# A dense feed-forward layer that takes 512 tokens at a time instead of 256

## The chip, the cores and the metric

The kernel runs on one core of a Trainium2 chip. The metric is the device time of one execution in microseconds (us); the kernel before has a median of 1231.29 us over three runs (1230.88 to 1233.56). Engines are named as in the profile: PE is TensorE (matmuls), PEld its weight loads, DVE is VectorE, ACT is ScalarE, POOL is GpSimd and SP is SyncE, whose queue issues most DMAs.

## What is computed

Attention over 4 x 8 heads (queries are first averaged in pairs) gives `x` with 2304 tokens of 512 numbers. A dense feed-forward layer follows, with w_in of 512 x 2048 and w_out of 2048 x 512, and then a layer of 8 experts in which each token goes to one:

```
h = x @ w_in
x = (h * cos(h)) @ w_out                      # dense feed-forward

expert = argmax(x @ w_gate);  p = softmax(x @ w_gate)[expert]
out = p * (relu(x @ w1[expert]) @ w2[expert])
```

## The kernel before, in words

Numbers are kept in float32 precision by splitting an operand into a high part (`xh`, rounded by a copy to the matmul's type) and a low part (`xl`, the rest). Each product is three matmuls: high by high, high by low, low by high. The splitting copy is done by ACT, the subtraction by DVE.

Three stages follow each other on PE: attention (to 480.83 us of the profile), the dense layer (to about 914), the experts (to about 1220). The attention leaves x transposed in SBUF (`xT`), as 9 chunks of 256 tokens, and converts w_in and w_out into their two parts, through memory (`ws`).

The dense layer is in `moe`. The outer loop takes a chunk `c` of 256 tokens, the inner loop `f` 16 slices of 128 of the 2048 hidden numbers. A step (c, f) is one `layer1`, and one `layer2` that lies four steps behind (LAG):

- `layer1` (L859): 12 matmuls of 256 moving columns into a PSUM bank `h` (four banks), the weights stationary, L870. Then a chain on ACT and DVE forms h cos(h): L875 scales and rounds on ACT, L876 to L878 reduce the argument on DVE, L879 takes a sine and L880 squares it on ACT, L881 multiplies by h on DVE, L882 (ACT) and L883 (DVE) split the result into `g`. `h` is read last by L881 and `g` is one of eight buffers. `a` and `r`, the values in between, share a 256 + 256 tile in SBUF.
- `layer2` (L886): 6 matmuls of 512 columns, L891, `g` stationary, into two PSUM banks `po` that collect the sum over the 16 steps.

Behind the last step of a chunk the `epilogue` runs in pieces, one piece a step: it copies `po` out (L804), transposes it on PE (L812), forms the expert scores (L820, L825) and lets the `Router` rank the tokens. In the last chunk the first expert's weights are converted as well (`conv`, L715 on ACT, L716 on DVE, 1024 columns each).

The text of the program is not the order of the instructions: the framework's scheduler moves them past each other on each engine within what data, buffers and its own estimates allow. Every engine then runs its own instructions strictly in the order so fixed, and waits where a semaphore tells it to.

The experts load raw weights through 9 buffers `raw` (L693, L706, L708), which in the earlier stages hold `xT`, convert them and multiply in `compute`.

Of the kernel before, what the change touches and what calls it, by code (L numbers as in the profile page):

```python
# [8 lines left out]
F32 = mybir.dt.float32  # L9
F32R = mybir.dt.float32r  # L10
# [3 lines left out]
AF = mybir.ActivationFunctionType  # L14
# [7 lines left out]
CH = 256  # L22
ROW = 512 + 8


# [151 lines left out]
def attention(nc, tc, q, k, v, xT, ident, w_in, w_out, ws, x2d, W1):  # L177
# [11 lines left out]
    with ExitStack() as ctx:  # L189
# [177 lines left out]
        def norm(i, hq):  # L367
            b, c = divmod(i, HP)
            t = t0 = b*SQ + hq*NQ
            o = T.pop(("ob", i, hq))  # L370
            while t < t0 + NQ:
                n = min(CH - t % CH, t0 + NQ - t)
                nc.gpsimd.tensor_mul(xT[t//CH][:, c, t % CH:t % CH+n], o[:, t-t0:t-t0+n], T["nr", i, hq][:, t-t0:t-t0+n])
                t += n
# [57 lines left out]
class Router:  # L432
# [51 lines left out]
    def bank(self, name):  # L484
        return self.ps.tile([128, 512], F32, tag="h", name=name)
# [163 lines left out]
def moe(nc, tc, magic, rp, xT, ws, w_gate, x2d, w1, w2, out, ident, W1, wp):  # L649
# [5 lines left out]
    NCH = NT // CH  # L655
    LAG = 4
    C1 = 6.28125
    C2 = 2 * math.pi - C1
    with ExitStack() as ctx:
        pool = lambda name, bufs, **k: ctx.enter_context(tc.tile_pool(name=name, bufs=bufs, **k))  # L660
        xhp = pool("xh", 3)
        xlp = pool("xl", 2)
        hp = pool("g", 8)
        op = pool("o", 4)
        wp = wp + [pool(f"w{j}", 1) for j in range(len(wp), FT)]
        cq = pool("cm", 1)
        gp = pool("gate", 3)
        x2p = pool("x2", 3)
# [3 lines left out]
        half = lambda name: ps_h.tile([128, 512], F32, tag="h", name=name)[:, :CH]  # L672
        bank = lambda name: ps_m.tile([128, 512], F32, tag="h", name=name)
# [9 lines left out]
        def xtiles():  # L683
            return [(xhp.tile([128, 2, CH], F32R, tag="xh", name="xh"), xlp.tile([128, 2, CH], F32R, tag="xl", name="xl")) for _ in range(KC // 2)]

# [7 lines left out]
        def load(i, part=range(8)):  # L693
            s = slots[i][1]
            src = router.e0 if i == 0 else router.eid[0:1, s:s+1]
            if part[0]:

                src = router.e1
                tc.keep_in_program_order(nc.gpsimd.tensor_copy(src, router.eid[0:1, s:s+1]))
            e = nc.sync.value_load(src, min_val=0, max_val=NE-1)  # L700
            RAW.setdefault(i, [])
            for j in part:
                t = rp.tile([128, 1024], F32, tag="raw", name="raw")
# [47 lines left out]
        def compute(i, between=()):  # L751
# [3 lines left out]
            if n == 2:  # L755
                for m in range(F2):
                    ph = half("ph")
# [5 lines left out]
                    h = hp.tile([128, 2, CH], F32R, tag="g", name="hh")  # L763
                    nc.scalar.activation(h[:, 0], ph, AF.Relu)
                    nc.vector.scalar_tensor_tensor(h[:, 1], ph, 0.0, h[:, 0], op0=ALU.max, op1=ALU.subtract)
                    hs.append(h)
            else:
                for u in range(2):
                    hr = otile("hr")
                    ph = ps_h.tile([128, 512], F32, tag="h", name="ph")  # L770
                    c = 0
                    for k in range(KC):
                        for a, y in ((0, 0), (0, 1), (1, 0)):
                            nc.tensor.matmul(ph, lhsT=x[k//2][y][:, k % 2, :128], rhs=wt[k][:, a, u*512:(u+1)*512], start=(c == 0), stop=(c == 3*KC-1))
                            c += 1
                    nc.scalar.activation(hr, ph, AF.Relu)
                    p = bank("ht")
                    for k in range(4):
                        nc.tensor.transpose(p[:, k*128:(k+1)*128], hr[:, k*128:(k+1)*128], ident)
                    for k2 in range(2):  # L780
                        h = hp.tile([128, 2, CH], F32R, tag="g", name="hh")
                        pv = p[:, k2*256:(k2+1)*256]
                        nc.scalar.copy(h[:, 0], pv)  # L783
                        nc.vector.tensor_sub(h[:, 1], pv, h[:, 0])
                        hs += [h[:, :, :128], h[:, :, 128:]]
            for q in range(n):
                po = ps_o.tile([128, D], F32, tag="po", name="po")
                c = 0
# [10 lines left out]

        def epilogue(c, po):  # L800
# [4 lines left out]
            yield  # L805
            if c < NCH-1:
                yield
            x2t = []
# [47 lines left out]

        tail, todo, xs, pos = [iter(())], [], {}, {}

        def layer1(c, f):  # L859
            if c == 0 and f >= EARLY:  # L860
# [4 lines left out]
            w, x = W1[f], xs[c]  # L865
            h = half("h")
            n = 0
            for k in range(KC):
                for a, y in ((0, 0), (0, 1), (1, 0)):
                    nc.tensor.matmul(h, lhsT=w[:, a, k*128:(k+1)*128], rhs=x[k//2][y][:, k % 2], start=(n == 0), stop=(n == 3*KC-1))  # L870
                    n += 1
            ar = op.tile([128, 2, CH], F32, tag="o", name="ar")
            a, r = ar[:, 0], ar[:, 1]
            g = hp.tile([128, 2, CH], F32R, tag="g", name="g")
            nc.scalar.activation(a, h, AF.Identity, bias=magic, scale=1.0/(2*math.pi))  # L875
# [8 lines left out]
            todo.append((c, f, g))  # L884

        def layer2(c, f, g):  # L886
            if f == 0:
                pos[c] = [ps_o.tile([128, D], F32, tag="po", name="po") for t in range(2)]
            for t in range(2):
                for i, (y, b) in enumerate(((0, 0), (0, 1), (1, 0))):  # L890
                    nc.tensor.matmul(pos[c][t], lhsT=g[:, y, t*128:(t+1)*128], rhs=W1[f][:, b, 512:], start=(f == 0 and i == 0), stop=(f == FT-1 and i == 2))  # L891
            if f == FT-1 and c < NCH-1:
                tail[0] = epilogue(c, pos.pop(c))

        xs[0] = xtiles()
        split_x(xs[0], xT[0])
        for c in range(NCH):
            for f in range(FT):
                layer1(c, f)
                while len(todo) > (LAG + 1 if f == LAG and c else LAG):  # L900
                    layer2(*todo.pop(0))
                next(tail[0], None)
                if c == 0 and f == 8:
                    router = Router(nc, cq, op, ps_m, NT // 128, NE)
                if c < NCH-1 and f == FT-2:
                    xs[c+1] = xtiles()
                    split_x(xs[c+1], xT[c+1])
                if c == NCH-1 and f >= 9:
                    conv(0, f - 9)
# [3 lines left out]
        split(0)  # L913
        for _ in epilogue(c, pos.pop(c)):
            pass
# [24 lines left out]
def body(nc, tc, q, k, v, w_in, w_out, w_gate, w1, w2, out):  # L940
    with ExitStack() as ctx:
# [9 lines left out]
        x2d = dp.tile([NT + 128, ROW], F32, name="x2d")  # L951
        rp = ctx.enter_context(tc.tile_pool(name="raw", bufs=NT // CH))
        xT = [rp.tile([128, 1024], F32, tag="raw", name="xT").rearrange("p (k n) -> p k n", n=CH) for c in range(NT // CH)]

# [43 lines left out]
```

## Time and profile before

| | us |
|---|---|
| median of 3 runs | 1231.29 |
| profiled execution | 1229.78 |
| its span, first to last instruction | 1228.1 |
| PE busy in the span | 1199.8 |
| DVE busy | 873.6 |
| ACT busy | 760.5 |
| POOL busy | 432.1 |

The difference between the profiled execution and its span, 1.7 us, lies around the first and last instruction. Busy time is counted per engine and engines overlap, so the shares do not add up to the span. The granted clock is 0.998 of full speed over the whole span. Within a stage, what matters is which engine has no idle time: a window of the trace tells that, and a timeline tells how far apart the instructions of a chain start. The chain that ended last goes back only to the last store and its issue (3 pieces), so it says nothing about the dense layer.

### The profile page before, as it was taken

What the parts mean: (1) busy time and instruction counts of PE and PEld (TensorE: products, weight loads), DVE (VectorE), ACT (ScalarE), POOL (GpSimd) and SP (SyncE); (2) the same over time, 40 slices, a digit from 0 to 9 for tenths busy, and PEclk for the clock granted to TensorE, in tenths of its full rate; (3) what the DMA queues carried; (4) which work ended last, traced back from release to release, by engine and by line L of the source; (5) the groups of instructions that cost most, each with busy time, mean ns of one, the idle gap of its engine ahead of it and who ended that gap; (6) DMA issues with size and microseconds to landing.
All of it is one profiled execution on the core that took longest, in us unless ns stands there. A gap on an engine that the chain in (4) does not pass through costs nothing. (4 is left out here: it accounts for less than half of the span.)

```text
span 1228.1 us, 22479 instructions
## 1 busy us (share of the span) xinstructions
PE 1199.8 (98%) x8286; PEld 937.3 (76%) x8286; DVE 873.6 (71%) x1895; ACT 760.5 (62%) x1528; POOL 432.1 (35%) x386
## 2 busy tenths in 40 slices
PE   5999999999999999999999999999998999999997
PEld 3566666666665556989889889889987888888886
DVE  4677777767777766767767767767777977777761
ACT  3566666666666666666566565565574877677751
POOL 4687888888888776000000000000003121112100
PEclk9999999999999999999999999999999999999999
DMA  6234464433433335600000000000047997779710
GB/s 257 74 95 147 176 221 147 151 128 127 127 132 108 118 105 223 258 19 1 18 19 1 19 1 18 19 1 19 21 153 256 399 328 267 271 274 313 259 58 7
DMA packets 70943, 163.74 MB, mean 133 GB/s; under 512 B 7669, under 2 KB 24813, under 8 KB 68784
## 3 DMA queue, kind: packets, MB, share of 16 engines
q1 hardware_dynamic: 66832, 150.92, 35.1%
q0 software_dynamic: 4000, 11.38, 2.5%
q8 instruction: 65, 1.06, 0.4%
q14 instruction: 46, 0.38, 0.1%
HBM read 135.65 MB, written 28.39 MB: 134 GB/s over the span
## 5 line engine op out<-in xcount | busy, mean ns | idle before, releaser
L334 POOL TENSOR_TENSOR es<-es,E 128x576 f32<-128x576 f32 x192 | 274.6, 1430 | 34.6 <-ACT E L327 24.6
L327 ACT ACTIVATE E<-s 128x576 f32<-128x576 f32 x288 | 183.4, 653 | 122.9 <-PE s L323 111.9
L870 PE MATMUL h<-xh,wf 128*128 128x256 f32 x1152 | 231.6, 285 | 0.5 <-DVE ar L881 0.5
L274 DVE TENSOR_REDUCE MX<-pmx 128x2 f32<-128x768 f32 x192 | 183.2, 957 | 68.4 <-PE pmx L263 68.4
L891 PE MATMUL po<-wf,g 128*128 128x512 f32 x864 | 222.3, 394 | 1.5 <-ACT g L882 0.9
L321 PE MATMUL s<-Q,K 64*128 64x288 f32 x1152 | 191.9, 417 | 1.5 <-ACT E L327 1.5
L870 PEld LDWEIGHTS h<-xh,wf 128*128 128x128 f32 x1152 | 188.1, 191 | 6.5 <-issue 1.8
L727 POOL DMA_INDIRECT xg<-x2d,idx x25 | 27.7, 1106 | 465.5 <-ACT ar L875 388.7
L891 PEld LDWEIGHTS po<-wf,g 128*128 128x128 f32 x864 | 153.4, 189 | 28.4 <-ACT g L882 1.6
L716 DVE TENSOR_TENSOR w<-raw,w 128x1024 fp32r<-128x1024 f32 x128 | 154.6, 1221 | 21.2 <-ACT w L715 15.5
L340 PE MATMUL o<-E,vt 128*64 128x288 f32 x1152 | 169.1, 417 | 0.2 <-ACT E L327 0.2
L870 PE MATMUL h<-xl,wf 128*128 128x256 f32 x576 | 163.0, 283 | 0.0
L323 PE MATMUL s<-MR,ON 64*128 64x288 f32 x576 | 148.4, 511 | 0.0
L715 ACT CAST w<-raw 128x1024 fp32r<-128x1024 f32 x128 | 132.9, 1053 | 20.1 <-DMA raw<-in_moe_w_dram 11.8
L794 PE MATMUL po<-w,hh 128*128 128x512 f32 x600 | 143.6, 392 | 0.4 <-ACT hh L783 0.3
L794 PEld LDWEIGHTS po<-w,hh 128*128 128x128 f32 x600 | 110.7, 188 | 22.6 <-ACT hh L783 0.8
L879 ACT ACTIVATE ar<-ar 128x256 f32<-128x256 f32 x144 | 59.9, 417 | 94.5 <-DVE ar L878 94.1
L340 PEld LDWEIGHTS o<-E,vt 128*64 128x64 f32 x1152 | 72.0, 136 | 59.9 <-issue 24.8
L321 PEld LDWEIGHTS s<-Q,K 64*128 64x128 f32 x1152 | 97.7, 188 | 25.2 <-issue 13.4
L870 PEld LDWEIGHTS h<-xl,wf 128*128 128x128 f32 x576 | 110.0, 191 | 3.7
L761 PE MATMUL ph<-xh,w 128*128 128x256 f32 x576 | 109.2, 286 | 1.2 <-ACT xh L688 1.2
L881 DVE SCALAR_TENSOR_TENSOR ar<-ar,h 128x256 f32<-128x256 f32 x144 | 60.2, 419 | 61.0 <-ACT ar L880 60.5
(200 smaller groups left out, 1808.0 us busy)
## 6 DMA issues: line engine op xcount, KB each, us to landing
raw<-in_moe_w_dram SPq DMA_DIRECT2D x128, 512.0 KB
wf<-ws SPq DMA_DIRECT2D x16, 1024.0 KB
vt<-in_v_dram SPq DMA_DIRECT2D x16, 576.0 KB
qr<-in_q_dram SPq DMA_DIRECT2D x15, 576.0 KB
K<-in_k_dram SPq DMA_DIRECT2D x15, 576.0 KB
cv_t<-in_moe_w_in_dram SPq DMA_DIRECT2D x16, 512.0 KB
ws<-cv_o SPq DMA_DIRECT2D x32, 256.0 KB
cv_t<-in_moe_w_out_dram SPq DMA_DIRECT2D x16, 512.0 KB
```

The source lines that it names most:

```text
L274: nc.vector.reduce_max(out.rearrange("p (w g) -> p w g", g=3)[:, 2*t:2*t+2, g], p[:, :, :KG], axis=AX.X)
L321: nc.tensor.matmul(p[:, h, :NQ], lhsT=T["k", i][R[h], j*128:(j+1)*128], rhs=T["q", i][R[h], qs], start=True, stop=False)
L323: nc.tensor.matmul(p[:, h, :NQ], lhsT=ON[R[h]], rhs=MR[i % 3][R[h], qs], start=False, stop=True)
L327: nc.scalar.activation(e, T.pop(("s", i, hq, j))[:, :, :NQ], AF.Exp, scale=1.0/16)
L334: nc.gpsimd.tensor_add(T["es", i, hq], T["e", i, hq, 0] if j == 1 else T["es", i, hq], T["e", i, hq, j])
L340: nc.tensor.matmul(T["o", i, hq][64*h:64*h+64], lhsT=T["v", i][:, h, j], rhs=T["e", i, hq, j][:, h], start=(j == 0), stop=(j == J-1))
L715: nc.scalar.copy(w[:, 0], t)
L716: nc.vector.tensor_sub(w[:, 1], t, w[:, 0])
L761: nc.tensor.matmul(ph, lhsT=wt[k][:, a, m*128:(m+1)*128], rhs=x[k//2][y][:, k % 2], start=(c == 0), stop=(c == 3*KC-1))
L794: nc.tensor.matmul(po, lhsT=hs[m][:, y, q*128:(q+1)*128], rhs=wt[4 + m//2][:, a, (m % 2)*512:(m % 2)*512+512], start=(c == 0), stop=(c == ...
L870: nc.tensor.matmul(h, lhsT=w[:, a, k*128:(k+1)*128], rhs=x[k//2][y][:, k % 2], start=(n == 0), stop=(n == 3*KC-1))
L891: nc.tensor.matmul(pos[c][t], lhsT=g[:, y, t*128:(t+1)*128], rhs=W1[f][:, b, 512:], start=(f == 0 and i == 0), stop=(f == FT-1 and i == 2))
```

## The change

The dense layer takes 512 tokens at a time: four passes `d` of 512, and one of 256 for the rest. `xT` is 4 tiles of 512 tokens and one of 256. A new `layer1` has 12 matmuls of 512 moving columns (8 with the high part, then 4 with the low part), a new `layer2` 12 of 512 columns into four `po` banks, and follows two steps behind instead of four (three in the last pass, and in part of the others). The number of `layer1` matmuls falls from 1728 to 960, 768 of which have 512 columns; `layer2` keeps its 864.

PSUM has 8 banks. The four `h` banks become two and the two `po` banks four. `r` moves from SBUF into the two banks of `ps_m`, which the epilogue and the router also use. `a` keeps a 512-column tile in SBUF. `g` is two tiles of twice 512 instead of eight of 256. The high part of x takes an 8 KB buffer of its own in the first and the last pass, and a raw buffer in the passes between. Splitting is done by two helpers, `high` (4 copies on ACT, L878) and `low` (4 subtractions on DVE, L886). Both epilogues of a pass go two pieces a step, three in the last pass, so that two of them fall in the 16 steps of the last pass. The nine raw buffers become four pairs and a rest of 4 KB. In the experts, the pools of `ph` and `po` swap places. Constants of the router now lie where the attention's converted weights `cv_o` lay, so the instructions that write them (on POOL, and one on DVE) wait for these weights' last stores.

```
-    LAG = 4
+    LAG = 2
-        xhp = pool("xh", 3)
-        xlp = pool("xl", 2)
-        hp = pool("g", 8)
+        xhp = pool("xh", 1)
+        xlp = pool("xl", 4)
+        hp = pool("g", 2)
-        ps_h = pool("ps_h", 4, space=PSUM)
-        ps_o = pool("ps_o", 2, space=PSUM)
+        ps_h = pool("ps_h", 2, space=PSUM)
+        ps_o = pool("ps_o", 4, space=PSUM)
...
+        def high(d):
...
+            n = xT[d].shape[2]
+            t = (rp if 0 < d < ND-1 else xhp).tile([128, KC, DC], F32R, tag="raw" if 0 < d < ND-1 else "xh", name="xh")[:, :, :n]
+            for k in range(KC):
+                nc.scalar.copy(t[:, k], xT[d][:, k])
+            return t
+        def low(d, xh):
+            n = xT[d].shape[2]
+            x = []
+            for k in range(KC):
+                x.append((xh[:, k], xlp.tile([128, DC], F32R, tag="xl", name="xl")[:, :n]))
+                nc.vector.tensor_sub(x[k][1], xT[d][:, k], xh[:, k])
+            return x
...
+        def layer1(d, f, x):
...
+            h = ps_h.tile([128, DC], F32, tag="h", name="h")[:, :N]
+            n = 0
+            for k, a, y in [(k, a, 0) for k in range(KC) for a in range(2)] + [(k, 0, 1) for k in range(KC)]:
+                nc.tensor.matmul(h, lhsT=w[:, a, k*128:(k+1)*128], rhs=x[k][y], start=(n == 0), stop=(n == 3*KC-1))
+                n += 1
+            a, r = otile("a")[:, :N], bank("r")[:, :N]
             nc.scalar.activation(a, h, AF.Identity, bias=magic, scale=1.0/(2*math.pi))
             nc.vector.tensor_scalar(a, a, MAGIC, None, op0=ALU.subtract)
             nc.vector.scalar_tensor_tensor(r, a, -C1, h, op0=ALU.mult, op1=ALU.add)
             nc.vector.scalar_tensor_tensor(r, a, -C2, r, op0=ALU.mult, op1=ALU.add)
             last["act"] = nc.scalar.activation(r, r, AF.Sin, scale=0.5).ins
-            nc.scalar.activation(r, r, AF.Square)
-            nc.vector.scalar_tensor_tensor(a, r, 0.5, h, op0=ALU.subtract, op1=ALU.mult)
+            nc.scalar.activation(a, r, AF.Square)
+            nc.vector.scalar_tensor_tensor(a, a, 0.5, h, op0=ALU.subtract, op1=ALU.mult)
             nc.scalar.copy(g[:, 0], a)
             last["dve"] = nc.vector.tensor_sub(g[:, 1], a, g[:, 0]).ins
...
+        x = low(0, high(0))
+        for d in range(ND):
+            for f in range(FT):
+                layer1(d, f, x)
+                if d < ND-1 and f == FT-4:
+                    xh = high(d+1)
+                if d < ND-1 and f == FT-1:
+                    x = low(d+1, xh)
+                while len(todo) > LAG + (f == LAG and d > 0 or d == ND-1):
+                    layer2(*todo.pop(0))
+                go_on(2 if d < ND-1 else 3)
+                if d == ND-1 and f >= 9:
+                    conv(0, f - 9)
```

The lines of the chain are L907 (the first on ACT, L875 before), L908 to L910 (DVE), L911 and L912 (ACT), L913 (DVE), L914 (ACT) and L915 (DVE); layer 1's matmuls are L900 and layer 2's L924, and the conversions L718 and L719.

PE in the middle of the dense layer, before: layer 1 of one step and layer 2 of another.

```order
L870 MATMUL h<-xl,wf 128x256
L870 MATMUL h<-xh,wf 128x256 x2
L870 MATMUL h<-xl,wf 128x256
L870 MATMUL h<-xh,wf 128x256 x2
L870 MATMUL h<-xl,wf 128x256
L870 MATMUL h<-xh,wf 128x256 x2
L870 MATMUL h<-xl,wf 128x256
L870 MATMUL h<-xh,wf 128x256
L891 MATMUL po<-wf,g 128x512 x7
```

And now, where the `layer2` of an earlier step follows each `layer1`:

```order
L900 MATMUL h<-xl,wf 128x512 x4
L924 MATMUL po<-wf,g 128x512 x12
L900 MATMUL h<-xh,wf 128x512 x8
L900 MATMUL h<-xl,wf 128x512 x4
L924 MATMUL po<-wf,g 128x512 x12
L900 MATMUL h<-xh,wf 128x512 x8
```

All matmuls of the middle passes have 512 columns, and the high part's eight come before the low part's four.

ACT where the dense layer starts, before. `ln` and `r` belong to the attention's last piece.

```order
L344 ACTIVATE ob<-o 128x288
L354 ACTIVATE ln<-psum,eps 128x288
L358 ACTIVATE r_5251<-ln 128x288
L875 ACTIVATE ar<-h,magic 128x256 x2
L879 ACT_TABLE_LOAD
L879 ACTIVATE ar<-ar 128x256 x2
L880 ACTIVATE ar<-ar 128x256 x2
L875 ACTIVATE ar<-h,magic 128x256
L882 CAST g<-ar 128x256
```

And now:

```order
L345 ACTIVATE ob<-o 128x288
L355 ACTIVATE ln<-psum,eps 128x288
L878 CAST xh<-xT 128x512
L359 ACTIVATE r_5234<-ln 128x288
L878 CAST xh<-xT 128x512 x3
L907 ACTIVATE a<-h,magic 128x512 x2
L911 ACT_TABLE_LOAD
L911 ACTIVATE r<-r 128x512
L912 ACTIVATE a<-r 128x512
L911 ACTIVATE r<-r 128x512
L912 ACTIVATE a<-r 128x512
```

Four copies for the next pass (L878) stand among and behind the attention's last ones, ahead of the first L907; before, none stood there.

DVE in the last pass, where the first expert's weights are converted, before:

```order
L876 TENSOR_SCALAR ar<-ar 128x256
L877 SCALAR_TENSOR_TENSOR ar<-ar,h 128x256
L878 SCALAR_TENSOR_TENSOR ar<-ar 128x256
L716 TENSOR_TENSOR w<-raw,w 128x1024
L883 TENSOR_TENSOR g<-ar,g 128x256
L716 TENSOR_TENSOR w<-raw,w 128x1024
L881 SCALAR_TENSOR_TENSOR ar<-ar,h 128x256
L876 TENSOR_SCALAR ar<-ar 128x256
L716 TENSOR_TENSOR w<-raw,w 128x1024
L883 TENSOR_TENSOR g<-ar,g 128x256
L877 SCALAR_TENSOR_TENSOR ar<-ar,h 128x256
L716 TENSOR_TENSOR w<-raw,w 128x1024
```

And now:

```order
L913 SCALAR_TENSOR_TENSOR a<-a,h 128x256 x2
L915 TENSOR_TENSOR g<-a,g 128x256
L719 TENSOR_TENSOR w<-raw,w 128x1024
L915 TENSOR_TENSOR g<-a,g 128x256
L908 TENSOR_SCALAR a<-a 128x256
L719 TENSOR_TENSOR w<-raw,w 128x1024
L909 SCALAR_TENSOR_TENSOR r<-a,h 128x256
L908 TENSOR_SCALAR a<-a 128x256
L910 SCALAR_TENSOR_TENSOR r<-a,r 128x256
L909 SCALAR_TENSOR_TENSOR r<-a,h 128x256
L719 TENSOR_TENSOR w<-raw,w 128x1024
L910 SCALAR_TENSOR_TENSOR r<-a,r 128x256
```

The conversions (L716, now L719) stand between links of the chain in both. Now L908 to L910 of two steps stand among them in turn.

## Rows read from the trace of the kernel before

**Rows 1.** From the page, TensorE's busy time, share and instructions in the whole span

```profile
PE 1199.8 (98%) x8286; PEld 937.3 (76%) x8286; DVE 873.6 (71%) x1895; ACT 760.5 (62%) x1528; POOL 432.1 (35%) x386
```

**Rows 2.** Windows of four stages: length, each engine's busy us (instructions), granted clock, DMA

```profile
480.83:530.00 49.17, 48.68 (x323) 44.65 (x322) 36.73 (x107) 31.52 (x78) 2.58 (x6) 1.00 0.60 251
530.00:855.77 325.77, 325.77 (x2200) 292.38 (x2200) 235.05 (x726) 195.91 (x477) 0.00 (x0) 1.00 0.03 13
905.00:925.00 20.00, 18.67 (x128) 16.47 (x129) 14.82 (x57) 11.39 (x29) 0.00 (x0) 1.00 0.07 28
925.00:975.00 50.00, 46.83 (x272) 40.63 (x271) 39.57 (x97) 33.40 (x57) 14.37 (x13) 0.97 0.89 333
```

**Rows 3.** Windows of one step inside the feed-forward stage, same columns

```profile
577.50:578.93 1.43, 1.43 (x13) 1.43 (x12) 0.74 (x3) 0.62 (x2) 0.00 (x0) 1.00 0.00 0
578.93:580.32 1.39, 1.39 (x8) 1.13 (x7) 1.06 (x4) 1.37 (x4) 0.00 (x0) 1.00 0.00 0
```

**Rows 4.** Window of L794 alone: length, matmul busy, weight-load busy, clock, DMA

```profile
960.05:969.58 9.53, 9.53 (x43) 7.70 (x41) 1.00 1.04 398
```

**Rows 5.** ACT's groups by line and shape: busy us, mean ns, idle before

```profile
L875 ACT ACTIVATE ar<-h,magic 128x256 f32<-128x256 f32 x144 | 68.2, 474 | 41.4 <-PE h L870 40.5
L879 ACT ACTIVATE ar<-ar 128x256 f32<-128x256 f32 x144 | 59.9, 417 | 94.5 <-DVE ar L878 94.1
L688 ACT CAST xh<-xt 128x256 fp32r<-128x256 f32 x50 | 17.8, 374 | 3.2 <-PE xt L735 2.0 <-DVE xl L689 1.1
L688 ACT CAST xh<-xT 128x512 fp32r<-128x512 f32 x18 | 10.8, 605 | 2.2 <-POOL Q L238 2.2
L804 ACT ACTIVATE x<-po 128x512 f32<-128x512 f32 x18 | 10.5, 595 | 0.9 <-PE po L891 0.9
```

**Rows 6.** DVE's groups by line and shape, same columns

```profile
L876 DVE TENSOR_SCALAR ar<-ar 128x256 f32<-128x256 f32 x144 | 42.3, 294 | 30.8 <-ACT ar L875 28.0
L877 DVE SCALAR_TENSOR_TENSOR ar<-ar,h 128x256 f32<-128x256 f32 x144 | 60.5, 420 | 4.2
L689 DVE TENSOR_TENSOR xl<-xt,xh 128x256 fp32r<-128x256 f32 x50 | 19.6, 418 | 8.8 <-PE ph L774 8.7
L689 DVE TENSOR_TENSOR xl<-xT,xh 128x512 fp32r<-128x512 f32 x18 | 12.4, 697 | 2.1 <-ACT xh L688 1.8
L716 DVE TENSOR_TENSOR w<-raw,w 128x1024 fp32r<-128x1024 f32 x128 | 154.6, 1221 | 21.2 <-ACT w L715 15.5 <-issue 3.9
```

**Rows 7.** Timeline of ACT and DVE, 479.5 to 490: start us, us, instruction

```profile
479.78 1.41 DVE L689 TENSOR_TENSOR xl<-xT,xh 128x512 fp32r<-128x512 f32 x2
481.49 0.45 ACT L358 ACTIVATE r<-ln 128x288 f32<-128x288 f32 x1
482.57 0.47 ACT L875 ACTIVATE ar<-h,magic 128x256 f32<-128x256 f32 x1 [0.64 <-PE h L870]
483.08 0.29 DVE L876 TENSOR_SCALAR ar<-ar 128x256 f32<-128x256 f32 x1
483.41 0.42 DVE L877 SCALAR_TENSOR_TENSOR ar<-ar,h 128x256 f32<-128x256 f32 x1
483.87 0.61 DVE L878 SCALAR_TENSOR_TENSOR ar<-ar 128x256 f32<-128x256 f32 x1
484.51 1.28 ACT L879 ACT_TABLE_LOAD   x1
485.80 0.72 ACT L879 ACTIVATE ar<-ar 128x256 f32<-128x256 f32 x2
```

**Rows 8.** Windows of 5 us in the first experts, columns as in Rows 2

```profile
935.00:940.00 5.00, 3.73 (x21) 2.74 (x20) 3.04 (x9) 4.11 (x8) 4.23 (x5) 1.00 0.79 253
940.00:945.00 5.00, 3.81 (x22) 3.09 (x19) 2.58 (x6) 2.35 (x7) 2.75 (x3) 1.00 1.02 360
945.00:950.00 5.00, 4.29 (x22) 4.12 (x23) 3.49 (x7) 3.37 (x8) 1.02 (x1) 0.66 1.04 413
```

More of the change, by code (lines that the diff above doesn't have):

```diff
@@ L683, in xtiles @@
         def xtiles():
-            return [(xhp.tile([128, 2, CH], F32R, tag="xh", name="xh"), xlp.tile([128, 2, CH], F32R, tag="xl", name="xl")) for _ in range(KC // 2)]
+            return [[xlp.tile([128, 2, CH], F32R, tag="xl", name="xe") for _ in range(2)] for _ in range(KC // 2)]
         def split_x(x, src, cols=slice(0, CH)):
@@ L702, in load @@
             for j in part:
-                t = rp.tile([128, 1024], F32, tag="raw", name="raw")
+                if j % 2 == 0:
+                    two = rp.tile([128, 2, 1024], F32, tag="raw", name="raw")
+                t = two[:, j % 2]
                 k = j % 4
@@ L756, in compute @@
                 for m in range(F2):
-                    ph = half("ph")
+                    ph = ps_o.tile([128, 512], F32, tag="po", name="ph")[:, :CH]
                     c = 0
@@ L855, in epilogue, with go_on @@
                 yield
-        tail, todo, xs, pos = [iter(())], [], {}, {}
-        def layer1(c, f):
-            if c == 0 and f >= EARLY:
+        tails, todo, pos = [], [], {}
+        def go_on(n):
+            while tails and n:
+                n -= 1
+                if next(tails[0], 1):
+                    tails.pop(0)
+        def high(d):
[12 more added lines that the diff above has]
+        def layer1(d, f, x):
+            if d == 0 and f >= EARLY:
                 W1.append(wp[f].tile([128, 2, 1024], F32R, tag="w", name="wf"))
@@ L864, in layer1 @@
                     nc.sync.dma_start(wg, w_gate.rearrange("(k p) e -> p k e", p=128))
-            w, x = W1[f], xs[c]
-            h = half("h")
+            w = W1[f]
+            N = xT[d].shape[2]
+            h = ps_h.tile([128, DC], F32, tag="h", name="h")[:, :N]
             n = 0
[L868 to L874, printed above, removed]
+            for k, a, y in [(k, a, 0) for k in range(KC) for a in range(2)] + [(k, 0, 1) for k in range(KC)]:
+                nc.tensor.matmul(h, lhsT=w[:, a, k*128:(k+1)*128], rhs=x[k][y], start=(n == 0), stop=(n == 3*KC-1))
+                n += 1
+            if f*N % DC == 0:
+                last["g"] = hp.tile([128, 2, DC], F32R, tag="g", name="g")
+            o = f*N % DC
+            g = last["g"][:, :, o:o+N]
+            a, r = otile("a")[:, :N], bank("r")[:, :N]
             nc.scalar.activation(a, h, AF.Identity, bias=magic, scale=1.0/(2*math.pi))
@@ L886, in layer2 @@
-        def layer2(c, f, g):
+            todo.append((d, f, g))
+        def layer2(d, f, g):
+            nt = g.shape[2] // 128
             if f == 0:
-                pos[c] = [ps_o.tile([128, D], F32, tag="po", name="po") for t in range(2)]
-            for t in range(2):
+                pos[d] = [ps_o.tile([128, D], F32, tag="po", name="po") for t in range(nt)]
+            for t in range(nt):
                 for i, (y, b) in enumerate(((0, 0), (0, 1), (1, 0))):
-                    nc.tensor.matmul(pos[c][t], lhsT=g[:, y, t*128:(t+1)*128], rhs=W1[f][:, b, 512:], start=(f == 0 and i == 0), stop=(f == FT-1 and i == 2))
-            if f == FT-1 and c < NCH-1:
-                tail[0] = epilogue(c, pos.pop(c))
@@ L895, in moe @@
-        xs[0] = xtiles()
-        split_x(xs[0], xT[0])
-        for c in range(NCH):
-            for f in range(FT):
-                layer1(c, f)
-                while len(todo) > (LAG + 1 if f == LAG and c else LAG):
+                    nc.tensor.matmul(pos[d][t], lhsT=g[:, y, t*128:(t+1)*128], rhs=W1[f][:, b, 512:], start=(f == 0 and i == 0), stop=(f == FT-1 and i == 2))
+            if f == FT-1 and d < ND-1:
+                p = pos.pop(d)
+                x2s = [rows(p[:2]), rows(p[2:])]
+                tails.extend(epilogue(2*d + c, x2) for c, x2 in enumerate(x2s))
@@ L913, in moe @@
         split(0)
-        for _ in epilogue(c, pos.pop(c)):
+        for _ in epilogue(NCH-1, rows(pos.pop(ND-1))):
             pass
@@ L951, in body @@
         x2d = dp.tile([NT + 128, ROW], F32, name="x2d")
-        rp = ctx.enter_context(tc.tile_pool(name="raw", bufs=NT // CH))
-        xT = [rp.tile([128, 1024], F32, tag="raw", name="xT").rearrange("p (k n) -> p k n", n=CH) for c in range(NT // CH)]
+        rp = ctx.enter_context(tc.tile_pool(name="raw", bufs=NT // DC))
+        rest = ctx.enter_context(tc.tile_pool(name="rest", bufs=1))
+        xT = [rp.tile([128, 2048], F32, tag="raw", name="xT").rearrange("p (k n) -> p k n", n=DC) for c in range(NT // DC)]
+        xT.append(rest.tile([128, 1024], F32, name="xT").rearrange("p (k n) -> p k n", n=NT % DC))
         wp = [ctx.enter_context(tc.tile_pool(name=f"w{j}", bufs=1)) for j in range(EARLY)]
```

37 lines of the change are left out of this document (18 added, 19 removed).

## The prediction

> **What bounds the kernel now.** I read the page first: TensorE (PE) is busy 98% of the span [rows 1]. Then the windows by stage [rows 2]: 0.5 us of idle PE at the start of the feed-forward stage (480.83 to 530), none from 530 to 855.77, 1.3 us where it hands over to the experts (905 to 925) and 3.2 us in the first experts (925 to 975). So nearly the whole stage is PE's own rate, and a gain must come from what one matmul costs. One step of the inner loop f (144 of them) is 1.43 us of layer 1 (12 matmuls of 256 columns) and 1.39 us of layer 2 (6 of 512), 2.82 together [rows 3] (the counts there include one or two from the edges of the window). Beside that PE ACT and DVE work 1.99 and 1.80 us of a step, so they are not the bound, but not far from it: what they do in a chain per step is the quantity to watch.
>
> **A. The matmuls, first four passes.** A column of 256 comes every 1.43/12 = 0.119 us. Where 512-column matmuls follow each other with no 256 between, 42 of them take 9.53 us, 0.227 each [rows 4]; the six in rows 3 take 0.232 because each set begins behind 256-column work. A new step of 512 tokens has 24 matmuls, all of 512 columns: 24 x 0.227 = 5.44 us, against 2 x 2.82 = 5.64. 64 such steps: **-12.8 us**. With 0.232 throughout it would be 5.56 and -5; I take 0.227, since the mixed order is gone. The last 256 tokens keep the old shapes. The routing matmuls between passes are as many as before.
>
> The Trainium skill ("TensorE: Matmul & The Clock Gate", section on the gap between back-to-back matmuls) gives N / 2.4 GHz plus about 2.5 ns per matmul. By it, 768 matmuls fewer would save 768 x 2.5 ns = 1.9 us in place of 12.8 (an estimate from that page). The rows contradict the size: at 256 and 512 columns the excess over N / 2.4 GHz is 0.012 and 0.014 us. The measurement decides.
>
> **B. The start.** Before, four h banks let PE run four steps of layer 1 ahead, and ACT reaches the first L875 at 482.57 [rows 7]. Now DVE needs four L886 of 0.70 [rows 6] from 479.8 to 482.6, twice what it had, and ACT's row order puts four copies for the *next* pass (L878, 0.605 each [rows 5]) before the first L907; the first of them writes into a buffer that is free only after the fourth L886. So on ACT: 482.6 + 0.61 + 0.45 (L359) + 3 x 0.53 = 485.2 for the first L907. The second must wait for h of step 1: 480.83 + 24 x 0.227 + 0.17 = 486.4, ends 487.1; table load 1.28 [rows 7] to 488.4; L911 and L912 of step 0 to 489.7, L913 to 490.4. With two h banks, layer 1 of step 2 can only start then; PE is ready at 486.3. Stall 4.1, against 0.5 before: **+3.6 us** (1 to 4.5: the lower end if ACT overlaps its copies with the wait, the upper with every duration in full).
>
> **C. The chain against the step.** In each step ACT and DVE now alternate strictly: L907, 908, 909, 910, 911, 912, 913, 914. At 256 columns the starts in rows 7 give 0.51, 0.33, 0.46 for the first links, that is each duration plus 0.034, and independent neighbours on ACT start about 0.09 before the first ends (two L879 in 0.72, not 0.83). For 512: L907 0.474 + 0.231 = 0.70 (the 0.231 is what L688 gains from 256 to 512 [rows 5]), L908 0.43, L909, 910 and 913 0.70 each (0.42 + 0.28 [rows 6]), L911 and L912 0.64 each, L914 0.605 less the overlap. Sum 5.03 + 7 x 0.034 = **5.27 us per step**, against PE's 5.44. The chain keeps up with 0.17 to spare; a nearest-row lower end is 5.1 (ACT slope of 0.2), an upper one 5.7 (r in PSUM dearer than in SBUF, no overlap at all). That is far less slack than before, so what is inserted counts. An h bank has to be free 8.2 us after its layer 1 ended (one layer 1 and two layer 2 of 2.72 each) and L913 is through 4.5 after it in the unhurried case, so a delay of up to 3.7 costs nothing, and is worked off at 0.17 a step. Between passes ACT gets four L812 of 0.595, four L878 of 0.605 and the copies of two epilogues, DVE four L886 of 0.70: 5 us and 3 us. Most of them fall into idle time of their engine (5.44 - 2.6 on ACT, 5.44 - 3.2 on DVE). Following the rows through a pass change with the start-to-start times gives 0.2 us of PE stall, with full durations 1.8; I take 1.2, three times: **+3.6 us** (0.6 to 6).
>
> **D. The last 256 tokens.** Here a step is 2.82 us of PE again, but two h banks are left and ACT and DVE still go through one step's chain after the other: 0.51 + 0.33 + 0.46 + 4 x 0.45 + 0.34 = 3.44 us. The 16 steps become 16 x 3.44 = 55 in place of 45, less what L907 of the next step does ahead of L914 in about half of them, plus the two epilogues that now both fall in these 16 steps and eight L719 of 1.22 us [rows 6] on a DVE that has no room left. Layer 1 ends 11 us later relative to the pass's start; the drain of layer 2 behind it is shorter (three steps wait instead of five, 1.39 and their chains each), which gives back 5. The experts begin 6 to 8 us later: **+7 us** (1 if two chains overlap as on a DVE with room, 16 with full durations).
>
> **E. Clock.** After two stretches with PE busy 3.73 and 3.81 of 5 us the granted clock was 0.66 over the next 5 us [rows 8], that is the lower level of 1.2 GHz for about 3.4 us, worth 1.7 us. B and D make stretches like that. In D, PE waits anyway. I take one drop, **+1.7** (0 to 5).
>
> **F. Experts.** Their instructions are the same; token loads and raw weights have 8 buffers in pairs where there were 9 singles, and ACT and DVE keep their work. I take 0 (-4 to +2; below nothing, as a later start lets the loads get ahead of the 3.2 us of idle PE in rows 2). GpSimd's constants for the router and one DVE memset now wait for the last stores of converted weights, but they are first used in step 8 of the first pass, 40 us on: 0.
>
> **Sum.** -12.8 + 3.6 + 3.6 + 7 + 1.7 + 0 = +3.1. The profiled execution has 1229.78 us, span 1228.1 and 1.7 around it, 1.5 below the median of 1231.29. On the median's scale: 1231.3 + 3.1 = **1234.4 us**.
>
> **The rivals.**
> Faster, by the same step on the other side (L907 to L915 in the last 16 steps): if ACT and DVE interleave two steps there, the step stays near PE's 2.82 and D is 1 in place of 7, and E falls away, since PE waits only at the start. Then -12.8 + 3.6 + 2 + 1 = -6, **1225**. It decides at a period of 2.9 us per step. For it: 256-column neighbours do overlap by 0.09 in rows 7, ACT's order has L907 ahead of L914 in half of the steps. Against: DVE already has 2.0 us of its own in each step, and the conversions of 1.22 on top. 28 in 100.
> Slower throughout: the chain takes longer than 5.44. At 5.7 each of 64 steps waits 0.26: 17 us in place of C, sum -12.8 + 17 + 3.6 + 7 + 1.7 = +16, **1247**. For it: the spare is 0.17, 3%, and no row shows Sin or the two scaled subtractions on a 512-column r in PSUM. Against: L804 (0.595) reads PSUM at 512 and is not slower than L688 (0.605) from SBUF. 17 in 100.
> A wash: the delay of the experts is absorbed there. PE loses 1.3 + 3.2 us in the windows 905 to 975 and 1.7 by the clock; with weights landed and converted earlier relative to PE, 4 of those go: -0.9, **1230**. 15 in 100.
> That the larger matmuls do not pay (by the floor that the page names): -1.9 in A, sum +14, **1245**. The rows speak against it: 2 in 100.
> My forecast: 38 in 100, its own range 1232 to 1240.
>
> **How the numbers follow.** Two of ten lie outside 1223 to 1246: the low end is the faster rival with C at its bottom, the high end the chain-bound one just short of 1247. A difference of 0.2%, 2.5 us, is what a measurement of this kernel can tell from none. Faster by more than that: the faster rival with 28, and 2 of the wash: 0.30. Within: 13 of the wash, and 9 of the forecast's lower edge: 0.22. Slower: 29 of the forecast, 17 and 2: 0.48.
>
> **What would show it.** A: layer 1 and layer 2 steps 5.44 apart in the middle of a pass, with PE busy the whole time. B: a PE wait near 486 for DVE's L913 of about 4 us. C: few waits of PE on L913 or L915 between passes, about 1 us each; waits in every step would show the chain-bound rival. D: in the last 16 steps, a period near 3.4 and PE waiting for L913, conversions L719 among what DVE does. E: a granted clock under 1 within 10 us of B or D. F: the idle PE of rows 2 between 925 and 975 no larger. Wrong at the root would be: no change of pitch, or PE idle in the middle of a pass.

## The result and the profile after

The changed kernel takes 1244.58 us (median of 6 runs, 1243.1 to 1246.28) against 1231.21 for the kernel before, a ratio of 1.0108 with a 95% interval of 1.0094 to 1.0122: slower by 13 us, where 3 were forecast. The profiled execution has 1244.96 us and a span of 1243.1, 15.0 more than before (whose profiled execution lies 1.4 below its median). From the page, the row that answers to [rows 1]:

```profile
PE 1199.6 (96%) x7518; PEld 901.5 (73%) x7518; DVE 845.3 (68%) x1577; ACT 712.2 (57%) x1274; POOL 431.7 (35%) x370
```

PE does as much as before (1199.6 against 1199.8 us; its overlapping matmuls make this busy time a poor measure of the saving) in a span that is longer: what was added is idle PE and PE at a lower clock. Cut at the same events in both traces (first matmul of layer 1, first of the last 256 tokens, last of layer 2), the windows show where. First the kernel before, PE alone: length, busy us (instructions), granted clock, DMA share, GB/s.

```profile
480.83:855.77 374.94, 374.45 (x2521) 1.00 0.11 44
855.77:913.90 58.13, 56.62 (x361) 1.00 0.26 92
913.90:1228.10 314.20, 303.49 (x1814) 0.99 0.67 238
```

The same for the changed kernel:

```profile
481.66:851.06 369.40, 365.38 (x1719) 0.99 0.11 43
851.06:921.20 70.14, 61.62 (x384) 0.95 0.23 83
921.20:1243.10 321.90, 306.70 (x1824) 0.99 0.66 232
```

The stage of the 2048 tokens is 5.5 us shorter, the last 256 tokens are 12.0 longer and the experts, which the change was not meant to touch, 7.7 longer. With 0.8 us by which the attention ended later in this execution, that is the 15.0. (The runs below begin the dense layer anywhere from 480.3 to 484.5; where it is 484.5, the granted clock fell for some 7 us near 400.)

The middle of the dense layer is what A and C spoke of. Two steps of the changed kernel in windows (columns as in [rows 2], to hold against [rows 3]), and the waits of PE between 500 and 850, of which there is none: PE is busy 350.00 of 350.00 us.

```profile
652.86:658.30 5.44, 5.44 (x26) 4.50 (x24) 3.20 (x6) 2.49 (x4) 0.00 (x0) 1.00 0.00 0
658.30:663.74 5.44, 5.44 (x26) 4.51 (x24) 3.98 (x8) 4.46 (x8) 0.00 (x0) 1.00 0.01 3
...
500.00:850.00 350.00, 350.00 (x1662) 283.88 (x1661) 227.16 (x473) 166.47 (x280) 1.13 (x3) 1.00 0.06 23
```

A step is 5.44 us, as forecast. But a whole middle pass keeps less than its steps promise. From step 14 of one pass to step 14 of the next, two chunks of 256 before and one pass of 512 in the changed kernel:

```profile
557.68:653.25 95.57, 95.57 (x648) 85.81 (x645) 68.92 (x213) 57.61 (x140) 0.00 (x0) 1.00 0.03 12
...
559.18:652.86 93.68, 93.68 (x454) 75.58 (x452) 61.50 (x133) 46.12 (x80) 0.00 (x0) 1.00 0.03 12
```

That is 1.9 us saved, where 16 steps at 5.44 in place of 5.64 would save 3.2. The missing 1.3 us are busy time of PE, not a wait. Most of them lie where the routing matmuls of two chunks (L531 to L554 and L820 to L838) stand among those of layer 1: in each pass 16 matmuls of layer 1, each next to one of them, take 0.31 to 0.35 us instead of 0.227, such as these two, which a routing matmul follows at 584.00:

```profile
583.34 0.73 PE L900 MATMUL h<-xh,wf 128*128 128x512 f32 x2
584.00 0.42 PE L833 MATMUL pq<-x2t,wg 128*32 128x128 f32 x8
```

Together the 16 lose 1.6 us a pass (1.1 were lost so in the two chunks before), and the routing matmuls themselves take 0.5 more, which makes about 1.0 of the 1.3. Why a matmul takes longer there was not tested.

How far the chain is from holding PE up is read from ACT's timeline (start, duration, instruction, and in brackets its idle time before and what ended it):

```profile
655.00 0.62 ACT L914 CAST g<-a 128x512 fp32r<-128x512 f32 x1 [0.81 <-DVE a L913]
655.78 0.69 ACT L907 ACTIVATE a<-h,magic 128x512 f32<-128x512 f32 x1 [0.16 <-PE h L900]
658.42 0.58 ACT L911 ACTIVATE r<-r 128x512 f32<-128x512 f32 x1 [1.95 <-DVE r L910]
```

L907 of a step waits 0.16 us for layer 1 after L914 of the step before it: that is the whole slack, and the forecast's 5.27 us for the chain, 0.17 short of 5.44, came from durations of other lines at 512 columns. The next rows are the waits of PE behind the attention in the changed kernel, all of them new or larger than before (total us, times, longest), and the windows around them:

```profile
PE h L900 <- DVE a L913: 12.5, 4, 5.0
PE ph L764 <- ACT hr L783: 3.9, 6, 0.7
PE ph L764 <- ACT xe L689: 3.1, 3, 2.4
PE ph L764 <- DVE xe L690: 1.0, 1, 1.0
```

```profile
480.83:500.00 19.17, 15.15 (x59) 11.64 (x56) 11.37 (x19) 10.46 (x18) 4.46 (x14) 0.82 1.00 416
850.00:890.00 40.00, 37.45 (x258) 32.10 (x257) 27.73 (x105) 19.00 (x45) 2.25 (x2) 1.00 0.18 64
890.00:910.00 20.00, 14.03 (x71) 11.93 (x70) 16.01 (x32) 12.22 (x23) 0.00 (x0) 0.83 0.44 164
930.00:1000.00 70.00, 65.82 (x393) 57.95 (x392) 55.54 (x127) 46.45 (x79) 16.55 (x14) 0.95 0.87 321
```

Of the 12.5 us on L913, 4.0 lie at the start and 8.5 in the last pass; and behind both, the granted clock of a window falls, to 0.82 over 19.17 us and 0.83 over 20 us. Each is worth 3.4 us with PE at work throughout (some 7 us at the lower level, 1.2 GHz); for part of that time PE was idle anyway. The waits of L764 are in the experts, where the clock falls a third time, to 0.95 over 70 us; before, it fell there for about half as long ([rows 8]: 0.66 over 5 us).

### The profile page after: what moved, and what is told of

It reads as the page before. It is cut to its first block, busy times and chain, and to the rows that moved or that the text cites. A ratio compares the mean times of both kernels' runs of the same rounds, so it can differ in the third digit from the quotient of the medians.

```text
span 1243.1 us, 20281 instructions
## 1 busy us (share of the span) xinstructions
PE 1199.6 (96%) x7518; PEld 901.5 (73%) x7518; DVE 845.3 (68%) x1577; ACT 712.2 (57%) x1274; POOL 431.7 (35%) x370
## 4 chain that ended last, share of the span: by engine, by line
PE 89%; issue 3%; ACT 3%; DMA 2%; DVE 2%; POOL 1%; SPq 0%; POOLq 0%; ACTq 0%; DVEq 0%
PE h L900 16%; PE po L924 15%; PE o L341 12%; PE s L322 12%; PE po L802 9%; PE ph L764 7%; PE pmx L264 5%; PE s L324 3%; PE psum L351 3%; PE ph L781 2%; PE pmx L267 1%; DMA raw<-in_moe_w_dram 1%; ACT w L718 1%; DVE MX L275 1%; PE pt L820 1%
## 5 line engine op out<-in xcount | busy, mean ns | idle before, releaser
L924 PE MATMUL po<-wf,g 128*128 128x512 f32 x864 | 211.1, 392 | 0.0
L924 PEld LDWEIGHTS po<-wf,g 128*128 128x128 f32 x864 | 161.8, 189 | 32.9 <-DVE g L915 0.2
L719 DVE TENSOR_TENSOR w<-raw,w 128x1024 fp32r<-128x1024 f32 x128 | 155.7, 1221 | 42.0 <-ACT w L718 40.3
L900 PE MATMUL h<-xh,wf 128*128 128x512 f32 (+1 forms) x640 | 154.5, 380 | 12.5 <-DVE a L913 12.5
L718 ACT CAST w<-raw 128x1024 fp32r<-128x1024 f32 x128 | 133.1, 1053 | 28.8 <-PE po L802 15.3
L900 PEld LDWEIGHTS h<-xh,wf 128*128 128x128 f32 x640 | 112.2, 192 | 36.3 <-DVE a L913 14.9
L764 PE MATMUL ph<-xe,w 128*128 128x256 f32 x864 | 116.8, 289 | 8.0 <-ACT hr L783 3.9
L764 PEld LDWEIGHTS ph<-xe,w 128*128 128x128 f32 x864 | 110.5, 195 | 12.0 <-ACT hr L783 5.2
L911 ACT ACTIVATE r<-r 128x512 f32<-128x512 f32 (+1 forms) x80 | 43.2, 540 | 122.8 <-DVE r L910 111.1
L806 POOL DMA_INDIRECT out_dram<-ob,idx x25 | 27.2, 1088 | 206.4 <-ACT ob L805 190.8
L264 PE MATMUL pmx<-KH,QH 64*128 64x384 f32 x384 | 83.5, 433 | 11.1 <-ACT QH L251 7.6
```

What stands on the lines that cost most here:

```text
L264: nc.tensor.matmul(p[:, h, :KG], lhsT=QH[R[h], t*128:(t+1)*128], rhs=KH[R[h], g*KG:(g+1)*KG], start=True, stop=True)
L719: nc.vector.tensor_sub(w[:, 1], t, w[:, 0])
L900: nc.tensor.matmul(h, lhsT=w[:, a, k*128:(k+1)*128], rhs=x[k][y], start=(n == 0), stop=(n == 3*KC-1))
L924: nc.tensor.matmul(pos[d][t], lhsT=g[:, y, t*128:(t+1)*128], rhs=W1[f][:, b, 512:], start=(f == 0 and i == 0), stop=(f == FT-1 and i == 2))
```

## The experiments

All eight runs are timed against the kernel before on the same chip. The first four change one thing in the changed kernel each, whose own ratio is 1.0108.

**Copies for the second pass later (start_later).**

```
-                    xh = high(d+1)
+                    with tc.issue_after(last["act"]) if d == 0 else ExitStack():
+                        xh = high(d+1)
```

> The changed kernel, with the four copies for the second pass (high(1)) queued on ACT behind the sine of step 12 of the first pass instead of ahead of the first L907. Theory (the start costs what it does because these copies stand ahead of the first link of the chain, and the clock falls behind the idle PE): the first L907 starts about 1.5 us earlier, PE's wait for L913 falls from 4.0 to about 2.6 us, the drop of the clock after it (0.82 in 480.8 to 500, 3.4 us) goes, together -1.4 to -4.8 us: 1240 to 1243. Rival (two h banks alone make the wait, as L913 of step 0 can't end before both L907 and the table load are through): the wait stays at 3.5 or more, clock as it was, 1244 to 1245.

Measured: 1242.07 us, ratio 1.0096 (1.0079 to 1.0112), not told apart from the changed kernel by time. By the trace, the wait at the start goes from 4.0 to 3.1 us, and the 2048 tokens take 367.7 us in place of 369.4. The changed kernel's start on ACT first, then this run's (timelines), then this run's window:

```profile
483.29 0.62 ACT L878 CAST xh<-xT 128x512 fp32r<-128x512 f32 x1 [1.01 <-DVE xl L886]
484.16 1.64 ACT L878 CAST xh<-xT 128x512 fp32r<-128x512 f32 x3
485.71 0.68 ACT L907 ACTIVATE a<-h,magic 128x512 f32<-128x512 f32 x1
488.13 1.28 ACT L911 ACT_TABLE_LOAD   x1
```

```profile
484.05 0.69 ACT L907 ACTIVATE a<-h,magic 128x512 f32<-128x512 f32 x1 [1.96 <-PE h L900]
484.75 1.28 ACT L911 ACT_TABLE_LOAD   x1
...
480.83:500.00 19.17, 16.07 (x64) 12.68 (x63) 11.65 (x20) 9.55 (x16) 4.00 (x8) 0.91 1.01 424
```

L907 starts 3.05 us behind the first matmul here (481.00) and 4.05 behind it (481.66) in the changed kernel. So the copies were worth 1 us, and the rival, two banks, keeps the larger part, 3.1 (the last run below takes it away with a third bank). The clock still fell, to 0.91. In other executions with the full 4.0 us of wait it was 0.82 or 0.91 as well, here in the next run's, so the length of the wait alone does not set the size of this drop:

```profile
480.83:500.00 19.17, 15.15 (x60) 12.00 (x59) 10.68 (x18) 11.05 (x19) 3.13 (x7) 0.91 1.01 424
```

**Four h banks in the last pass (last_pass_banks).**

```
-            h = ps_h.tile([128, DC], F32, tag="h", name="h")[:, :N]
+            if d == ND-1 and f == 4:
+                last["hx"] = [ps_o.tile([128, D], F32, tag="po", name="hx") for t in range(2)]
+            if d == ND-1 and f >= 4 and f % 4 > 1:
+                h = last["hx"][f % 2][:, :N]
+            else:
+                h = ps_h.tile([128, DC], F32, tag="h", name="h")[:, :N]
```

> The changed kernel, with four h banks instead of two in the last pass from its fifth step on (two of the four po banks are free there). Theory (the last pass is long because a new layer 1 waits for L913 of two steps before): PE's waits for L913 after 850 fall from 8.5 us to 2 or less, the drop of the clock (0.83 in 890 to 910, 3.4 us) goes, layer 1 of the last pass ends 52 to 55 us after its first matmul instead of 64.4, the kernel at 1234 to 1238. Rival (the weight conversions, which wait for their DMA at the head of ACT's row, hold up every link behind them whatever number of banks): the waits move from h to g, same sum, 1243 to 1245.

Measured: 1235.61 us, ratio 1.0038 (1.0025 to 1.0051), 9 us better. All of PE's waits from 848 to 921 in this run:

```profile
PE po L929 <- ACT g L919: 1.3, 2, 0.8
PE h L905 <- DVE a L918: 0.7, 1, 0.7
PE ph L764 <- ACT xe L689: 0.3, 1, 0.3
```

8.5 us on L913 became 0.7, and 1.3 moved to g. Layer 1's last matmul starts 56.7 us after the pass's first in place of 64.4, a little later than expected. The clock of 890 to 910 is 0.91: its drop is half as large, where it was expected to go. The theory holds. The experts, which this edit does not touch, take 2.5 us less (319.2 in place of 321.8 from the end of the last layer 2), with a granted clock of 1.00 from 930 to 1000 in place of 0.95: part of what the experts lost came from the last pass.

**Conversions last (conversions_last).** To see what makes the chain late in that pass, the first expert's eight conversions stand behind the chain's last sine (on ACT) and last subtraction (on DVE):

```
-                if d == ND-1 and f >= 9:
-                    conv(0, f - 9)
...
-        conv(0, 7)
+        with tc.issue_after(last["act"]), tc.issue_after(last["dve"]):
+            for j in range(8):
+                conv(0, j)
```

> The changed kernel with the first expert's eight weight conversions queued behind the chain's last sine instead of from step 9 of the last pass on. Theory (with two banks, a conversion that waits for its DMA at the head of ACT's row holds the chain and so PE): the 5.0 us wait for L913 in 890 to 900 goes, layer 1 of the last pass ends 55 to 58 us after its first matmul in place of 64.4, and the clock stays up; but the first expert then waits for its weights, 8 x 1.2 us on DVE, some 8 us, so that the whole is 1243 to 1248. Rival (the chain itself is too slow for two banks, as I predicted, 3.4 us a step): layer 1 still ends 61 us or more after.

Measured: 1243.74 us, ratio 1.0133 (1.0106 to 1.016; three executions between 1243.1 and 1243.8, one of 1252.32), no gain over the changed kernel. Layer 1's last matmul starts 56.6 us after the first; of the waits on L913 in the pass, one is left:

```profile
PE h L900 <- DVE a L913: 2.5, 1, 2.5
...
890.00:910.00 20.00, 20.00 (x124) 17.75 (x123) 13.21 (x37) 11.42 (x30) 0.00 (x0) 1.00 0.42 154
910.00:930.00 20.00, 13.01 (x74) 11.39 (x73) 13.97 (x32) 13.21 (x24) 0.00 (x0) 0.74 0.02 5
```

The gain is spent in the next window: by the trace the first expert waits there for its split tokens `xe` (4.6 us on ACT's part, then 2.4 on DVE's), which stand behind the eight conversions in both rows, and the clock falls to 0.74. So the 5.0 us wait needs the conversions (and, by the run before, the two banks). In the changed kernel, ACT and then PE in that place:

```profile
892.38 1.04 ACT L718 CAST w<-raw 128x1024 fp32r<-128x1024 f32 x1 [1.38 <-DMA raw<-in_moe_w_dram]
895.13 1.04 ACT L718 CAST w<-raw 128x1024 fp32r<-128x1024 f32 x1 [1.71 <-DMA raw<-in_moe_w_dram]
896.08 0.37 ACT L911 ACTIVATE r<-r 128x256 f32<-128x256 f32 x1
```

```profile
897.37 1.86 PE L900 MATMUL h<-xh,wf 128*128 128x256 f32 x7 [5.00 <-DVE a L913]
```

Two L718 at the head of ACT's row wait 1.38 and 1.71 us for raw weights, with the L911 queued behind them whose data were ready (L910 on DVE ended at 892.81); PE waits 5.00 us for L913 of that step. Without the conversions, and with two banks, PE runs from 890 to 910 with no idle time: the chain of 3.44 us per step that I had put in D is not what bounds it. The remaining 2.5 us wait, before 890, has the router's small operations on DVE ahead of the chain; no run moves them.

**A second set for half of the tokens (experts_x_twice).**

```
-            return [[xlp.tile([128, 2, CH], F32R, tag="xl", name="xe") for _ in range(2)] for _ in range(KC // 2)]
+            xe = [xlp.tile([128, 2, CH], F32R, tag="xl", name="xe") for _ in range(2)]
+            two = rest.tile([128, 2, 2, CH], F32R, tag="rest", name="xe")
+            return [xe, [two[:, 0], two[:, 1]]]
```

(`rest`, the 4 KB of the last 256 tokens, is handed to `moe` for this.)

> The changed kernel, with a second set of buffers for half of an expert's split tokens, in the 4 KB that held the last 256 tokens. Theory (the experts are slower by 0.9 us in each pair of slots because the tokens of the next slot can't be split before the slot in work has read its own: one set where there was one and a half): the 36.7 us of a pair go back to 35.8, in 6 to 7 pairs -6 us, 1238 to 1240. Rivals (the order in which the buffers of hh come free; or weights that arrive in pairs): 36.7 stays, 1244 to 1245.

Measured: 1240.41 us, ratio 1.007 (1.0057 to 1.0083). The experts take tokens in slots, in turn a large one of 256 and a small one of 128. A small and a large slot together are the distance between two starts of the small slot's first layer (L774 before, L781 after, L783 here). Timelines of PE, the changed kernel:

```profile
1017.76 1.63 PE L781 MATMUL ph<-w,xe 128*128 128x512 f32 x6
...
1054.49 1.86 PE L781 MATMUL ph<-w,xe 128*128 128x512 f32 x7
```

This run:

```profile
1017.98 1.40 PE L783 MATMUL ph<-w,xe 128*128 128x512 f32 x5
...
1053.78 1.40 PE L783 MATMUL ph<-w,xe 128*128 128x512 f32 x5
```

36.73 us became 35.80, what the kernel before has (1007.22 to 1043.02); all waits on hr are gone, and the experts take 316.4 us in place of 321.8 (from the end of the last layer 2). What happened in the changed kernel, and in this run, when the large slot's tokens are split, on ACT:

```profile
1022.44 0.64 ACT L689 CAST xe<-xt 128x256 fp32r<-128x256 f32 x2
1024.40 0.66 ACT L689 CAST xe<-xt 128x256 fp32r<-128x256 f32 x2
```

```profile
1018.91 0.65 ACT L691 CAST xe<-xt 128x256 fp32r<-128x256 f32 x2
1024.56 0.63 ACT L691 CAST xe<-xt 128x256 fp32r<-128x256 f32 x2
```

With the spare buffers the first copy of the next slot's tokens runs at 1018.91, beside the small slot's first layer; without them only at 1022.44, when that layer has read its own. PE then stands between the third and fourth matmul of L764 in the changed kernel:

```profile
1023.33 0.52 PE L764 MATMUL ph<-xe,w 128*128 128x256 f32 x3
1024.57 1.09 PE L764 MATMUL ph<-xe,w 128*128 128x256 f32 x7 [0.72 <-ACT hr L783]
```

This wait was put down to `hr`, which ACT had in its row next to the copy; the cause was the copy's missing buffer.

**One set in the kernel before (before_one_x_set).** The same from the other side:

```
-        xhp = pool("xh", 3)
+        xhp = pool("xh", 2)
```

> The kernel before with two xh buffers instead of three, so that an expert's split tokens have one set, as in the changed kernel. Theory: a pair of expert slots takes 36.7 us instead of 35.8, 6 to 7 pairs, +5 to +6: 1236 to 1237. The dense layer splits a chunk while the one before is still read, and has its own wait then, up to 1 us per chunk: up to 1244. Rival (the pairs of raw buffers make the 0.9 us): no change in the pairs, 1231.

Measured: 1237.43 us, ratio 1.0055 (1.0042 to 1.0068). The starts of two small slots, and the wait that the kernel before does not have:

```profile
1011.17 0.48 PE L774 MATMUL ph<-w,xh 128*128 128x512 f32 x1
...
1047.89 0.48 PE L774 MATMUL ph<-w,xh 128*128 128x512 f32 x1
```

```profile
PE ph L761 <- ACT hr L776: 3.6, 5, 0.7
```

36.72 us: one buffer of 2 KB fewer makes the whole difference of a pair, with single raw buffers and the old hh in place. The experts take 4.7 us more than before; 3.7 of the span's 8.5 lie ahead of the dense layer, where the granted clock was 0.77 from 395 to 410 in this execution. The rival with the pairs of raw buffers falls. The dense layer, where the theory allowed a loss, lost nothing (375.1 against 374.9 us).

**The order of hh, the expert's split hidden numbers (experts_hh_order).**

```
-                    if m in (0, 2):
+                    if m in (4, 6):
                         some = hp.tile([128, 2, 2, CH], F32R, tag="g", name="hh")
-                    elif m == 4:
+                    elif m == 0:
                         some = xhp.tile([128, 4, 2, CH], F32R, tag="xh", name="hh")
-                    h = some[:, m % (4 if m > 3 else 2)]
+                    h = some[:, m % (4 if m < 4 else 2)]
```

> The changed kernel, with a large slot's first four hh in the 8 KB buffer and the last four in the two g buffers, the other way round than now. Theory of this run (the g buffers are those that the small slot before used, so the large slot's first relu waits for that slot's second layer, and PE for the bank): a pair of slots falls from 36.7 to about 35.8 us, 1238 to 1240. Rival, which I hold for likelier (the one set of token buffers): no change, 36.7 and 1244 to 1245.

Measured: 1243.17 us, ratio 1.0105 (1.0089 to 1.0121); a pair of slots takes 36.73 us as before the edit. No effect, as the rival said.

**Three edits at once, and the start (all_three, all_three_and_start).** The first has the edits of start_later, last_pass_banks and experts_x_twice. The second gives step 2 of the first pass a third bank, one of `po`, and starts layer 2 one step later there:

```
-                h = ps_h.tile([128, DC], F32, tag="h", name="h")[:, :N]
+                h = (ps_o.tile([128, DC], F32, tag="po", name="hx") if d == 0 and f == 2 else ps_h.tile([128, DC], F32, tag="h", name="h"))[:, :N]
...
-                while len(todo) > LAG + (f == LAG and d > 0 or d == ND-1):
+                while len(todo) > LAG + (f == LAG or d == ND-1):
```

> The changed kernel with three edits of the runs before it at once: the copies for the second pass behind step 12's sine, four h banks in the last pass, the second set of token buffers in the experts. Theory (the three losses lie in different stretches and add up): from 1244.6, the sum of the three separate gains -2.5 -9.0 -4.2, so 1228 to 1230, within 0.2% of the kernel before. Rival (what is given back in the last pass is lost again in the experts, whose weights then come too late): 1232 to 1235, with idle PE between 930 and 1000 larger than the 3.2 us of before.

> As the run with all three edits, and step 2 of the first pass writes its h into one of the po banks, with the first layer 2 one step later, so that PE has four layers 1 to do before it needs anything of the chain. Theory (two h banks are what is left of the wait at the start): the wait of 3.1 us falls to about 1, the clock stays up between 481 and 500 (1.7 to 3.4 us), together -2 to -5 against the run with three edits: 1224 to 1227, faster than the kernel before. Rival (the wait only moves to the first layer 2, which needs g, and to its fourth bank): the sum of waits in 481 to 505 stays at 3 or more, 1228 to 1230.

Measured: 1227.38 us, ratio 0.9976 (0.9966 to 0.9987), and 1223.86 us, ratio 0.9951 (0.9938 to 0.9964). The losses add up as expected, and the second version beats both kernels. Its start, in the same window as above:

```profile
480.83:500.00 19.17, 18.79 (x86) 14.55 (x85) 14.87 (x26) 11.18 (x19) 4.99 (x17) 1.00 0.99 407
...
PE h L907 <- DVE a L920: 0.4, 1, 0.4
```

One wait of 0.4 us is left of 4.0, PE is busy 18.79 us in place of 15.15, and the clock stays at its upper level: the 2048 tokens take 363.5 us against 374.9 before, 11.4 less. Not all of that comes from the larger matmuls: the routing matmuls of one chunk, some 2 us of PE, now run in the last 256 tokens, which take 62.7 us here against 58.3 before. That leaves some 9 us.

## Why the prediction was right in sign and short in size

- **A** held in the step: 5.44. The 512-column rows of the experts were the right rows, and the 0.232 of the mixed step the wrong ones. It did not hold in the pass, which saves 1.9 us and not 3.2, so of the -12.8 the stage keeps some 9. By the Trainium skill's rule ("TensorE: Matmul & The Clock Gate", the gap between back-to-back matmuls) it would have been 1.9 us in all, an estimate from that page; the trace decides against that size.
- **B** held: 4.1 us of stall forecast, 4.0 measured, by the links foreseen: L907 4.05 us behind the first matmul, the table load behind the second L907 (488.13), L913 of step 0 before layer 1 of step 2. Of what makes it, though, the copies are 1 us and the banks 3.
- **C** came near in its number by luck: +3.6 forecast as waits of PE for the chain, and there is no PE wait at all between 500 and 850. The chain's 5.27 us was right. What three changes of passes do cost, 1.3 us each, is busy time of PE around the routing matmuls, of which the forecast said only that they are as many as before.
- **D** had the right place and too low a price: +7 forecast, 12.0 measured with the clock in it, where 7 and 1.7 were foreseen. 7.0 of the 12.0 are idle PE (8.5 us against 1.5), 5.0 busy time: the routing matmuls of one more chunk, and matmuls at the lower clock. The step that failed is the period of 3.44 us per step. There was no such period: PE ran at its own pace except in three waits of 2.5, 5.0 and 1.0 us, the largest behind conversions that waited for their DMA. That the conversions stand in DVE's way I had counted; that they wait, at the head of ACT's row, for data that have not landed, I had not.
- **E** was mis-sized: one drop of 1.7 us forecast, three windows measured, each worth some 3.4 with PE at work throughout and less where it is idle. At the start the run with a third bank takes 5.9 us off the 2048 tokens, 3.6 of them wait, so the clock cost about 2 there; the third window is in the experts, where the kernel before has half as much.
- **F** failed outright: 0 forecast with +2 as its upper end, 7.7 measured. 4.3 lie between the first and the last small slot: six distances, five of which went from 35.8 to 36.7 us, while the first was 36.85 before. 3.4 lie ahead of the first small slot, where the clock alone explains some 1.7; most of this part went with the waits of the last pass (last_pass_banks), and the rest stays open. "Their instructions are the same" was true and beside the point. The diff shows the cause of the 4.3: the old tiles of split tokens came from three xh and two xl buffers, the new ones from four xl in all, four being one slot's need. I had followed the buffers of the dense layer one by one and those of the experts only for raw and hh.

So the sum, +3.1, missed the 15.0 of the two spans by F 7.7, by D with the clock behind it 3.3 (12.0 against 8.7) and by 0.8 of the attention. For the 2048 tokens it was right, -5.6 forecast by A, B and C and -5.5 measured, but that is luck too: the clock's 2 us at the start were not in these terms, and the routing matmuls of a chunk, as much again, left this stage. The measured 1244.58 lies outside the forecast's own 1232 to 1240, and inside the whole range only because the range takes in the slower rival. The slower rival, a chain-bound step at 1247, came close to the time for a reason that is nowhere in the trace: its 0.26 us of wait in every step is not there. The faster rival fell with D. The wash did not happen: PE is idle 4.2 of the 70 us from 930 to 1000 (before, 3.7 from 922.8 to 992.8), and the clock falls there for longer. The three costs that the runs gave back come from buffers, not from the larger matmul: two banks in two places and one set of tokens.

## What to carry to other kernels

When a change lays memory out anew, list each pool's buffers per use before and after, in every stage that draws on it, those too whose code only changes a pool's name; the loss here sat in a stage that kept all its instructions. Give a stage with slack its few buffers, and look for free ones (a bank not yet or no longer in use) at its first and last steps, where the slack is gone. A gain per step is to be checked over a whole pass, with the other work that stands between the steps. And an instruction that waits for a DMA holds up everything behind it on its engine, so it is worth asking, before it is moved into a chain, when its data land.

## What the runs showed of the hardware

The clock falls in unlike amounts behind like waits: with the same 4.0 us wait at the start the granted clock of 480.8 to 500 was 0.82 in two profiled executions and 0.91 in three others. The 2048 tokens took 369.4 and 369.9 us in the two and 368.6 to 368.7 in the three, so one profile can be about 1 us off on this alone. Behind 0.4 us of wait it was 1.00. In a stream of 512-column matmuls with nothing between them, one follows another every 0.227 us; the six of a set that stands between 256-column work take 0.232 each. Where the routing matmuls stand between them, 16 matmuls of layer 1 in a pass took 0.31 to 0.35, and this is busy time by the profile: a stretch without a single wait of PE gave 1.3 us less in each pass than its steps promised.
